# Zero products in TensorE's gaps, two product buffers in one tile, and one statistic for four heads, in cosine attention followed by a low-rank mixer

## The chip, the core and the metric

One core of one Trainium2 chip runs the kernel. The metric is the device time of one execution in microseconds, median of three runs: 604.58 us before (604.14 to 604.91). The core's engines work side by side, each through its own list of instructions in order: PE (TensorE: products and transposes), ACT (ScalarE), DVE (VectorE), POOL (GpSimd) and SP (SyncE); POOL and SP here issue most of the transfers. Semaphores order the engines among each other. PE writes its products to a memory of its own, PSUM, which has eight banks of 2 KB in each of 128 partitions.

## What is computed

Inputs q, k and v are (8, 12, 448, 64): batches, heads, tokens, width. The attention normalises q and k, and its output goes, heads side by side as 768 channels, through a low-rank mixing of tokens and a two-layer MLP on channels:

```python
q_n = q / (norm(q) + 1e-06);  k_n = k / (norm(k) + 1e-06)
scores = q_n @ k_n.T / tau
attn = softmax(scores)
x = (attn @ v) with the heads side by side        # (8, 448, 768)
u = x + (x.T @ U @ V).T                           # U: 448 x 32, V: 32 x 448
out = u + relu(u @ w_ch1) @ w_ch2                 # 768 -> 3072 -> 768
```

## The kernel before

Heads are taken in pairs, six pairs (0 to 5) in a batch, eight batches. In this text heads are also counted through all batches: head 12 is the first of batch 1. For each pair:

- Squares and sums (`squares`: ACT L455 or DVE L457, then DVE L461) give the squared norms of q and k. A logarithm and an exponential (ACT L474 and L477), an addition and a reciprocal (DVE L480 and L482) make the inverse norms. `stats` does this for a group of heads together; a group's small instructions wait for all of its sums.
- `norm` scales q and k (DVE L536, tile `xn`). In batches 0 and 1 PE transposes the result (L374, tile `tp`), twelve transposes a pair, eight of keys and four of queries, and ACT or DVE copies it to `qkT` (L826 or L828). From batch 2 on a transfer transposes.
- `attention` makes seven score products (PE L572) in three PSUM buffers `sc`, seven exponentials (ACT L577, tile `attn`), and for each head sixteen products with v (PE L594), four groups of four, which go to the PSUM buffer `av`. A column of ones in v makes the sums of the softmax. DVE takes their reciprocal (L601, tile `rd`) and multiplies (L603) into `X_sb`.

`av` is a ring of two buffers: a head takes the buffer of the head two back.

`stage0` mixes tokens (L625 to L700), and `mlp` does the two dense layers (L762 and L796, with relu at L785 and L787), whose products fill PE between those of the attention of the next batches.

The order of instructions is made by a planner in the kernel's own Python. Every operation is an `Op` with an engine, an expected duration, its dependencies, the ring slots that it takes and frees, and a priority. `Plan.run` walks through time, and gives a free engine the first operation that is ready: on PE and POOL from several streams, tried in the order in which they were made; on ACT, DVE and SP by priority. An `"ACT/DVE"` operation goes to whichever is free. The operations are then emitted in order of their planned starts, and waits between engines are put in by the framework below, from what each instruction reads and writes in each tile. The planner's durations are thus estimates that set an order; they do not appear in the program.

In the first pair the planner takes longer durations for PE: 0.31 for a score product (L572), 0.09 for a product with v (L594), 0.09 for a transpose (L557), where later ones have 0.19, 0.033 and 0.05. The start runs through `first`, `second`, `third` and `fourth`: loads of heads 0 to 2, 2 to 4, 4 to 8 and 8 to 12 of batch 0. The heads of `third` have two groups of statistics, 4 to 6 and 6 to 8 (L907 and L908).

Of the kernel before, what the change touches and what calls it, by code (L numbers as in the profile page):

```python
# [10 lines left out]
FP = mybir.dt.float32  # L11
BF = mybir.dt.bfloat16
# [192 lines left out]
def kernel(  # L205
# [12 lines left out]
    nc = tc.nc  # L218

    B, H, S, D = q.shape  # L220
# [11 lines left out]
    EPS = 1e-6  # L232
    PE_BATCHES = 2
    LATE, VLATE = 8.0, 3.2

    const = ctx.enter_context(tc.tile_pool(name="const", bufs=1))
    pool = ctx.enter_context(tc.tile_pool(name="pool", bufs=1))
    psum = ctx.enter_context(tc.tile_pool(name="psum", bufs=1, space=bass.MemoryType.PSUM))
# [8 lines left out]
    def ring(n, shape, dt, name, space=None):  # L247
        p = space or pool
        return Ring(n, lambda i: p.tile(shape, dt, name=name, tag=name, bufs=n))

    def fixed_ring(tiles):
        return Ring(len(tiles), lambda i: tiles[i % len(tiles)])
# [39 lines left out]
    r_rd = ring(2, [128, 4, 1], FP, "rd")  # L292
    r_mm = ring(3, [128, 512], FP, "mm", psum)
    r_sc = ring(3, [128, 512], FP, "sc", psum)
    r_av = ring(2, [128, 4, D + 8], FP, "av", psum)


    U_sb = const.tile([128, 2, 4, R], BF, name="U_sb")
    V_sb = const.tile([128, PAD + S + PAD], BF, name="V_sb")
    ident = const.tile([128, 128], BF, name="ident")  # L300
    w1_sb = const.tile([128, CC, F], BF, name="w1_sb")

    nc.scalar.preload_act_table_set("natural_log_exp_and_others")
# [13 lines left out]
    plan = Plan()  # L317
# [3 lines left out]
    pe_a = plan.stream("PE")  # L321
    pe_sc = plan.stream("PE")
    pe_mlp = plan.stream("PE")
    pool_q = plan.stream("POOL")

    def pe_t(n):
        return n / 2400.0 + 0.0025
# [14 lines left out]
    def fill(fn, n=256, prio=8, acq=(), deps=()):  # L342
        return plan.add(Op("DVE", 0.05 + n * 0.0005, fn, deps=deps, acq=acq, prio=prio))
# [46 lines left out]
    got, last_exp = {}, {}  # L390
# [95 lines left out]
    def stats(b, h0, h1, ld, ops, lo, hold=(), then=()):  # L486

        pr = 0.3 + 0.03 * h0 if b == 0 else 4
        inv = Slot(r_inv, h1 - h0)
        o, _ = scales(b, h0, h1, ld, ops, lo, (0, 1), inv, pr, "DVE" if b else "ACT/DVE", hold, then)  # L490
        for p in range(h0 // 2, h1 // 2):
            o_ = norm(b, p, ld, lo + 2 * p - h0, inv, 2 * p - h0, {0: o, 1: o}, pr)
        return o_
# [22 lines left out]
    def norm(b, p, ld, la, inv, a, deps, pr):  # L516


        by_pe = b < PE_BATCHES
        first = b == 0 and p == 0  # L520
        xn, qkT = Slot(r_xn, 3 if first else 2 if by_pe else 1), Slot(r_qkT, 7)
        need = [xn_set[count[0] % len(xn_t)]]
        count[0] += 1

        def part(i, h0=0, h1=2):
            def fn():
                n = h1 - h0
                src = ld.tile[:, i, la + h0:la + h1, :].rearrange("p h (c d) -> p h c d", d=D)
                sc = inv.tile[:, i, a + h0:a + h1, :].unsqueeze(3).to_broadcast([SCH, n, SC, D])
                if i == 0:  # L530
                    dst = xn.tile[:, 8:12, :].rearrange("p c (h d) -> p h c d", h=2)
                else:
                    dst = xn.tile.rearrange("p b e -> p (b e)")[:, 0:9 * 128].rearrange(
                        "p (h x) -> p h x", h=2)[:, h0:h1, 0:SC * 128].rearrange(
                        "p h (c e) -> p h c e", c=SC)[:, :, :, 0:D]
                nc.vector.tensor_mul(dst, src, sc)  # L536
            return plan.add(Op("DVE", dve_t(256 * (h1 - h0)), fn, deps=need + [deps[i]], acq=[xn],
                               rel=[getattr(ld, "slot", ld), inv], prio=pr))

        if first:  # L540
            ops = [part(0), part(1, 0, 1), part(1, 1, 2)]
            blocks = [(8, 12, ops[0]), (0, 4, ops[1]), (4, 8, ops[2])]
        else:
            ops = [part(1), part(0)]
            blocks = [(0, 8, ops[0]), (8, 12, ops[1])]
        if not by_pe:
            done = [plan.add(Op("SP", 0.1, lambda: nc.sync.dma_start_transpose(
                out=qkT.tile, in_=xn.tile.rearrange("p b e -> p (b e)")), deps=ops, acq=[qkT],
                rel=[xn], prio=0, lat=("x", 0.05 * 84, LATE)))]
        else:  # L550
            done = []
            for b0, b1, o in blocks:
                done.append(flip(
                    pe_tp, [(lambda z=z: xn.tile[:, z, :]) for z in range(b0, b1)], SCH,
                    lambda: qkT.tile, (lambda t_, x, b0=b0, b1=b1: key_tiles(t_, x, b0 // 4, b1 // 4)
                                   if b == 0 and b0 < 8 else [(t_[:, b0:b1, :], x)]),
                    [o], [qkT], [xn], 1, "ACT/DVE", 0.09 if first else 0.05, b == 0 and b0 < 8))  # L557
        got[b, p, "qkT"] = (qkT, lambda m: (done[:2] if m < 3 else done) if first else done, done)
        return ops


    def attention(b, p, X):
        off = PAD * (b % 2)
        qkT, qdeps, _ = got.pop((b, p, "qkT"))
        attn = Slot(r_attn, 2)
        exps = {}
        for m in (0, 1, 2, 6, 3, 4, 5) if b == 0 else range(7):
            sc = Slot(r_sc, 1)

            def score(sc=sc, m=m):  # L570
                kT = qkT.tile[:, 0:8, :].rearrange("p b s -> p (b s)")
                nc.tensor.matmul(out=sc.tile[:, 0:S], lhsT=kT[:, 128 * m:128 * (m + 1)],  # L572
                                 rhs=qkT.tile[:, 8:12, :].rearrange("p c s -> p (c s)"),
                                 start=True, stop=True)
            o = plan.add(Op("PE", 0.31 if b == 0 and p == 0 else pe_t(S), score, deps=qdeps(m), acq=[sc], rel=[qkT]),
                         pe_first if b == 0 else pe_sc)
            exps[m] = plan.add(Op("ACT", act_t(S), lambda sc=sc, m=m: nc.scalar.activation(  # L577
                out=attn.tile[:, m, off:off + S], in_=sc.tile[:, 0:S], func=AF.Exp,
                scale=inv_tau), deps=[o], acq=[attn], rel=[sc], prio=0.1 if b == 0 else 1))
        last_exp[b] = exps[5]  # L580
        if b == 0 and p == 0:
            last_exp["first"] = [exps[1]]
        muls = []
        for hh in range(2):
            h = 2 * p + hh
            av, rd = Slot(r_av, 1), Slot(r_rd, 1)
            mine = [3 * hh, 3 * hh + 1, 3 * hh + 2, 6] if b == 0 else [4 * hh, 4 * hh + 1, 4 * hh + 2, 3]
            need = [exps[m] for m in mine]
            for t in range(4):
                for j in range(4):  # L590
                    first, last = t == 0 and j == 0, t == 3 and j == 3
                    def fn(t=t, j=j, h=h, mine=mine, av=av):
                        m = mine[j]
                        nc.tensor.matmul(  # L594
                            out=av.tile[:, t, 0:D + 1],
                            lhsT=attn.tile[:, m, 128 * t:128 * (t + 1)],
                            rhs=v_t[b % 2][:, h, j, 0:D + 1], start=(j == 0), stop=(j == 3))
                    o = plan.add(Op("PE", 0.09 if b == 0 and p == 0 else 0.033, fn,
                        deps=need + got[b, h, "v"] + attn_set + [v_set[b % 2]] if first else (), acq=[av] if first else [],
                        rel=[attn] if last else []), pe_av)  # L600
            r = plan.add(Op("DVE", 0.20, lambda av=av, rd=rd: nc.vector.reciprocal(  # L601
                out=rd.tile, in_=av.tile[:, :, D:D + 1]), deps=[o], acq=[rd], prio=1))
            muls.append(plan.add(Op("DVE", dve_t(256), lambda av=av, rd=rd, h=h: nc.vector.tensor_mul(  # L603
                X.tile[:, :, h * D:(h + 1) * D], av.tile[:, :, 0:D],
                rd.tile.to_broadcast([128, 4, D])), deps=[r],
                acq=[X], rel=[av, rd], prio=1)))
        last_av[b, p] = o
        return muls
# [258 lines left out]
                       in_=V_f().rearrange("r (s c) -> r c s", c=SC))  # L867


    w2_ops = []  # L870
    NW = 4
    THIRDS = [(0, 4), (4, 8), (8, 12)]
# [6 lines left out]
    def att(b):  # L879
# [7 lines left out]
    first = lead, [plan.add(Op("SP", 0.45, lambda i=i, src=src: nc.sync.dma_start(  # L887
        out=lead.tile[:, i], in_=src[0, 0:2].rearrange("h (s c) d -> s h (c d)", c=SC)),
        acq=[uv], prio=-5, lat=2.5)) for i, src in enumerate((q, k))]
    second = load_qk(0, 2, 4, uses=2)  # L890
    third = load_qk(0, 4, 8)
# [7 lines left out]
    begun_2 = stats(0, 2, 4, *second, hold=begun[:2], then=begun)  # L899
# [4 lines left out]
    v0 = [plan.add(Op("SP", 0.45, lambda t=t: nc.sync.dma_start(out=V_f()[R * t:R * (t + 1)], in_=moe_V),  # L904
                      deps=[zf, *begun], prio=-2, lat=12.0)) for t in range(4)]
    u1 = load_u(1)
    stats(0, 4, 6, *third, hold=last_exp["first"], then=begun_2)  # L907
    stats(0, 6, 8, *third[:2], 2, hold=last_exp["first"], then=begun_2)  # L908
    late = stats(0, 8, 12, *fourth)
    load_w1(0, 6)  # L910
    load_w1(6, 12)
# [71 lines left out]
```

## Time and profile before

| what | us |
|---|---|
| median of three runs | 604.58 |
| the profiled execution, its own time | 604.58 |
| its span, first to last instruction | 602.7 |
| PE idle before its first instruction | 7.14 |
| first exponential of pair 0 (ACT L577) | 10.12 |
| first exponential of pair 2 | 20.47 |
| first product with v of head 4 | 29.84 |
| last exponential of batch 0 ends | 37.50 |
| dense products of line 762 start to run without a gap | 40.94 |
| last product with v (head 95) | 432 |

The rows of the groups by line for the two reads of `av`, and what ended the idle time before them:

```profile
L601 DVE RECIPROCAL rd<-av 128x4 f32<-128x4 f32 x96 | 17.0, 179 | 37.8 <-PE av L594 37.0
L603 DVE TENSOR_TENSOR X_sb<-av,rd 128x256 bf16<-128x256 f32 x96 | 40.1, 420 | 1.6
```

A row reads: line, engine, operation, what it writes and reads with shapes, how often; busy time in us and mean of one in ns; idle time of the engine just before, and what ended most of it. In a timeline a row is start, duration, engine, line, operation and how many are merged; in brackets the idle time before it and what ended it. In the chain of waits each row is start, duration and what the chain lay on. The page's clock row is the granted TensorE clock in tenths.

### The profile page before, as it was taken

The numbers are of one execution on the slowest core, as the hardware profiler recorded it, in microseconds if no ns is written. First come the engines' busy times: TensorE is split into PE (matmuls) and PEld (weight loads), VectorE is DVE, ScalarE is ACT, GpSimd is POOL, SyncE is SP. The second block draws the span as 40 slices with busy tenths as digits, with TensorE's granted clock in tenths as the row PEclk, the third lists the DMA queues.
The fourth block names the chain that finished last, engine by engine and source line by source line (L and its number), as shares of the span: only waits on it lengthen the run. The fifth ranks groups of instructions, "written<-read, shape, count | busy, mean of one in ns | idle before, by whom it ended". The sixth has DMA issues, their size and how long they took to land.

```text
span 602.7 us, 11511 instructions
## 1 busy us (share of the span) xinstructions
PE 584.3 (97%) x4702; PEld 346.8 (58%) x4725; DVE 300.8 (50%) x729; ACT 278.2 (46%) x601; POOL 114.9 (19%) x175
## 2 busy tenths in 40 slices
PE   4899999999999999999999999999999999999997
PEld 2566766555565665666445666566545666654465
DVE  8979849999988987654721244014300210110011
ACT  7867752477874377316741067505642025014300
POOL 8246334062703406000600000000000000000000
PEclk9999999999999999999999999999999999999999
DMA  9999999999998969715922142030002110310021
GB/s 134 201 181 118 202 202 121 166 132 144 148 173 114 180 105 147 111 53 94 121 27 66 53 73 47 1 93 27 15 1 53 52 40 1 89 43 1 0 53 54
DMA packets 150165, 54.81 MB, mean 91 GB/s; under 512 B 115040, under 2 KB 150112, under 8 KB 150112
## 3 DMA queue, kind: packets, MB, share of 16 engines
q0 software_dynamic: 72864, 25.73, 39.3%
q1 hardware_dynamic: 77184, 28.32, 25.8%
q8 instruction: 37, 0.61, 0.4%
q14 instruction: 16, 0.13, 0.1%
q10 hardware_dynamic: 64, 0.02, 0.0%
HBM read 52.25 MB, written 11.01 MB: 105 GB/s over the span
## 4 chain that ended last, share of the span: by engine, by line
PE 92%; DVE 4%; ACT 2%; issue 1%; DMA 0%; ACTq 0%
PE mm L796 36%; PE mm L762 34%; PE sc L572 10%; PE av L594 8%; PE mm L686 1%; DVE xn L536 1%; DVE ss L461 1%; ACT attn L577 1%; PE tp L374 1%; PE mm L651 1%; DVE qkT L828 1%; DMA raw_uv<-in_q_dram 0%; PE sc L762 0%; ACT relu L785 0%; PE sc L686 0%
## 5 line engine op out<-in xcount | busy, mean ns | idle before, releaser
L762 PE MATMUL mm<-uT,w_sb 128*128 128x384 bf16 (+1 forms) x1112 | 236.9, 353 | 1.2 <-ACT relu L785 0.2
L796 PE MATMUL mm<-w_sb,relu 128*128 128x384 bf16 (+1 forms) x1368 | 231.9, 324 | 0.3 <-DVE O_sb L805 0.3
L577 ACT ACTIVATE attn<-sc 128x448 bf16<-128x448 f32 x336 | 164.7, 547 | 108.9 <-PE av L594 55.5
L796 PEld LDWEIGHTS <-relu 128*128 128x128 bf16 x1368 | 132.6, 98 | 86.5 <-issue 0.2
L762 PEld LDWEIGHTS <-w_sb 128*128 128x128 bf16 x1152 | 112.1, 98 | 103.9 <-issue 1.4
L785 ACT ACTIVATE relu<-mm 128x512 bf16<-128x512 f32 (+1 forms) x158 | 86.6, 548 | 129.0 <-PE mm L762 128.3
L805 DVE TENSOR_TENSOR O_sb<-mm,u_nat 128x384 f32<-128x384 f32 (+1 forms) x57 | 31.1, 549 | 210.8 <-PE mm L796 207.5
L572 PE MATMUL sc<-qkT 128*128 128x448 bf16 x336 | 104.4, 361 | 3.9 <-ACT qkT L826 1.8
L594 PEld LDWEIGHTS <-attn 128*128 128x128 bf16 x1536 | 61.7, 98 | 16.9 <-issue 2.5
L418 POOL DMA_DIRECT2D v_nat<-in_v_dram x98 | 63.2, 656 | 32.6 <-DMA w_sb<-in_moe_w_ch_dram 15.6
L594 PE MATMUL av<-v_nat,attn 128*128 128x65 bf16 x1536 | 65.3, 194 | 0.5 <-DVE X_sb L603 0.5
L461 DVE TENSOR_REDUCE ss<-sq 112x8 f32<-112x512 bf16 x96 | 63.2, 673 | 0.4 <-ACT sq L455 0.3
L536 DVE TENSOR_TENSOR xn<-qk_nat,inv 112x512 bf16<-112x512 bf16 x94 | 61.0, 681 | 1.3 <-DMA qkT<-xn 1.1
L396 POOL DMA_DIRECT2D qk_nat<-in_q_dram x24 | 17.2, 716 | 134.6 <-DVE xn L536 73.0
L603 DVE TENSOR_TENSOR X_sb<-av,rd 128x256 bf16<-128x256 f32 x96 | 40.1, 420 | 1.6
L572 PEld LDWEIGHTS <-qkT 128*128 128x128 bf16 x336 | 28.3, 98 | 21.8 <-issue 5.6
L601 DVE RECIPROCAL rd<-av 128x4 f32<-128x4 f32 x96 | 17.0, 179 | 37.8 <-PE av L594 37.0
L457 DVE TENSOR_TENSOR sq<-qk_nat 112x512 bf16<-112x512 bf16 x87 | 33.6, 413 | 0.0
L700 DVE TENSOR_TENSOR u_nat<-mm,X_sb 128x384 bf16<-128x384 f32 x36 | 19.1, 552 | 14.4 <-PE mm L686 14.2
L787 DVE TENSOR_SCALAR relu<-mm 128x384 bf16<-128x384 f32 (+1 forms) x31 | 18.7, 604 | 12.7 <-PE mm L762 12.2
L474 ACT ACTIVATE ln<-ss 112x32 f32<-112x32 f32 (+2 forms) x27 | 6.4, 235 | 30.2 <-DVE ss L461 30.1
L374 PE MATMUL tp<-ident,xn 112*128 112x112 bf16 x144 | 11.6, 227 | 7.9 <-DVE xn L536 7.5
(61 smaller groups left out, 169.8 us busy)
## 6 DMA issues: line engine op xcount, KB each, us to landing
qk_nat<-in_q_dram POOLq DMA_DIRECT2D x23, 224.0 KB, 5.6
qk_nat<-in_k_dram POOLq DMA_DIRECT2D x23, 224.0 KB, 6.9
w_sb<-in_moe_w_ch_dram POOLq DMA_DIRECT2D x4, 1152.0 KB, 14.2
w_sb<-in_moe_w_ch_dram POOLq DMA_DIRECT2D x8, 576.0 KB, 16.6
out_dram<-O_sb SPq DMA_DIRECT2D x15, 168.0 KB, 2.3
out_dram<-O_sb SPq DMA_DIRECT2D x16, 144.0 KB, 2.1
out_dram<-O_sb SPq DMA_DIRECT2D x16, 120.0 KB, 2.0
out_dram<-O_sb SPq DMA_DIRECT2D x16, 96.0 KB, 2.2
```

What stands on the lines that cost most here:

```text
L418: nc.gpsimd.dma_start(out=vb[p0:p0 + s1 - s0, hs, j, 0:D], in_=v[b, hs].rearrange("h (s c) d -> c s h d", c=SC)[c, s0:s1]),
L457: nc.vector.tensor_mul(y, x, x)
L461: lambda i=i, a0=a0, a1=a1, sq=sq: nc.vector.reduce_sum(ss.tile[:, i, a0:a1, :].rearrange("p h c -> p (h c)"), sq.tile[:, 0:a1 - a0, :].re ...
L536: nc.vector.tensor_mul(dst, src, sc)
L572: nc.tensor.matmul(out=sc.tile[:, 0:S], lhsT=kT[:, 128 * m:128 * (m + 1)], rhs=qkT.tile[:, 8:12, :].rearrange("p c s -> p (c s)"), start=T ...
L577: exps[m] = plan.add(Op("ACT", act_t(S), lambda sc=sc, m=m: nc.scalar.activation(out=attn.tile[:, m, off:off + S], in_=sc.tile[:, 0:S], fu ...
L594: nc.tensor.matmul(out=av.tile[:, t, 0:D + 1], lhsT=attn.tile[:, m, 128 * t:128 * (t + 1)], rhs=v_t[b % 2][:, h, j, 0:D + 1], start=(j == ...
L603: muls.append(plan.add(Op("DVE", dve_t(256), lambda av=av, rd=rd, h=h: nc.vector.tensor_mul(X.tile[:, :, h * D:(h + 1) * D], av.tile[:, :, ...
L762: o = plan.add(Op("PE", pe_t(n), lambda cc=cc: nc.tensor.matmul(out=mm.tile[:, 0:n], lhsT=w1_sb[:, cc, f * 128:(f + 1) * 128], rhs=uT.tile ...
L785: nc.scalar.activation(out=relu.tile[:, f, 0:n], in_=mm.tile[:, 0:n], func=AF.Relu)
L796: nc.tensor.matmul(out=mm.tile[:, 0:c1 - c0], lhsT=relu.tile[:, f, i * 128:(i + 1) * 128], rhs=w2_t[:, f, c0:c1], start=(f == 0), stop=(f ...
L805: nc.vector.tensor_add(out=O.tile[:, 0:w], in0=mm.tile[:, 0:w], in1=us[i].tile[:, c0:c1]),
```

## The change

Three things are changed.

1. The two `av` buffers, so far two tiles of a ring, become the two halves of one tile of two banks. A head still takes the half of the head two back.
2. A tile `warm` of zeros is set by DVE, and 75 products of it with itself, 208 columns wide, are given to PE in a stream of their own, tried last: they are planned wherever no other stream is ready. They write the unused tail of the second bank. At the same time the longer durations of the first pair leave the plan.
3. Heads 4 to 8 of batch 0 have one group of statistics in place of two.

```diff
     LATE, VLATE = 8.0, 3.2
+    WARM = 75
...
-    r_av = ring(2, [128, 4, D + 8], FP, "av", psum)
+    av_t = psum.tile([128, 2, 512], FP, name="av", tag="av", bufs=1)
+    r_av = fixed_ring([av_t[:, i, 0:4 * (D + 8)].rearrange("p (t d) -> p t d", t=4) for i in range(2)])
...
+    warm = const.tile([128, 208], BF, name="warm")
...
+    pe_warm = plan.stream("PE")
...
-                    [o], [qkT], [xn], 1, "ACT/DVE", 0.09 if first else 0.05, b == 0 and b0 < 8))
+                    [o], [qkT], [xn], 1, "ACT/DVE", 0.05, b == 0 and b0 < 8))
...
-            o = plan.add(Op("PE", 0.31 if b == 0 and p == 0 else pe_t(S), score, deps=qdeps(m), acq=[sc], rel=[qkT]),
+            o = plan.add(Op("PE", pe_t(S), score, deps=qdeps(m), acq=[sc], rel=[qkT]),
...
-                    o = plan.add(Op("PE", 0.09 if b == 0 and p == 0 else 0.033, fn,
+                    o = plan.add(Op("PE", 0.033, fn,
...
+    warm_set = fill(lambda: nc.vector.memset(warm, 0.0), 100, prio=-9)
+    for i in range(WARM):
+        plan.add(Op("PE", 0.18, lambda i=i: nc.tensor.matmul(
+            out=av_t[:, 1, 304:512], lhsT=warm[:, 0:128], rhs=warm, start=(i == 0), stop=True,
+            skip_group_check=True), deps=[warm_set]), pe_warm)
...
-    stats(0, 4, 6, *third, hold=last_exp["first"], then=begun_2)
-    stats(0, 6, 8, *third[:2], 2, hold=last_exp["first"], then=begun_2)
+    stats(0, 4, 8, *third, hold=last_exp["first"], then=begun_2)
```

In the order that this gives, 36 of the 75 zero products stand ahead of the first transpose, and the last one just before the transposes of pair 2. The order of instructions on each engine is another one up to the end of batch 0's attention, and again the same as before from the dense products on, but for a few swaps in batch 1. POOL and SP keep their order throughout. The lines of the changed kernel that are named in this text are four further down up to the new products: L594 is L598 there, L601 and L603 are L605 and L607.

## The prediction

> **What bounds the kernel now.** I read the busy shares first, then the groups by line, the chain of waits, the timeline of the first 45 us, and last the timeline around each place where a head's product is read. TensorE is the bound as a whole.
>
> ```profile
> PE 584.3 (97%) x4702; PEld 346.8 (58%) x4725; DVE 300.8 (50%) x729; ACT 278.2 (46%) x601; POOL 114.9 (19%) x175
> PEclk9999999999999999999999999999999999999999
> ```
>
> PE is idle for 602.7 − 584.3 = 18.4 us, 7.14 of them before its first instruction. So later on whatever holds PE is paid in full. The clock row claims full speed throughout, but the durations do not:
>
> ```profile
> 8.90 1.30 PE L572 MATMUL sc<-qkT 128*128 128x448 bf16 x3 [0.26 <-ACT qkT L826]
> 12.43 1.32 PE L374 MATMUL tp<-ident,xn 112*128 112x112 bf16 x12
> 18.41 0.56 PE L374 MATMUL tp<-ident,xn 112*128 112x112 bf16 x8
> 20.08 0.73 PE L572 MATMUL sc<-qkT 128*128 128x448 bf16 x3 [0.59 <-ACT qkT L826]
> ```
>
> Up to 18 us PE is slow: a score product takes 0.37 us on the chain of waits up to 17.5 us and 0.19 from 31.92 on; transposes go from 0.10 each, (1.32 − 0.23) / 11, to 0.05, (0.56 − 0.19) / 7. Only a part of this slow stretch lies on the chain:
>
> ```profile
> 14.67 1.30 PE sc L572 x3
> 16.47 0.37 PE sc L572
> 19.00 0.76 DVE qkT L828 x3
> ```
>
> From 14.67 to 18.98 the chain lies on PE (4.3 us); before and after it lies on ACT and DVE. That bounds what a faster PE can give. Three marks of this stage are used below:
>
> ```profile
> 16.73 1.29 DVE L536 TENSOR_TENSOR xn<-qk_nat,inv 112x512 bf16<-112x512 bf16 x2
> 20.47 1.42 ACT L577 ACTIVATE attn<-sc 128x448 bf16<-128x448 f32 x3
> 29.84 1.18 PE L594 MATMUL av<-v_nat,attn 128*128 128x65 bf16 x32 [0.19 <-DVE X_sb L603]
> ```
>
> They are pair 2's normalised operands, pair 2's first exponentials, and head 4's product with v. Then the place that decides, here at the start of batch 5 (heads are counted through, 12 a batch; this is head 60 on):
>
> ```profile
> 266.98 1.18 PE L594 MATMUL av<-v_nat,attn 128*128 128x65 bf16 x32
> 267.70 0.18 DVE L601 RECIPROCAL rd<-av 128x4 f32<-128x4 f32 x1
> 267.91 0.42 DVE L603 TENSOR_TENSOR X_sb<-av,rd 128x256 bf16<-128x256 f32 x1
> 268.25 0.17 DVE L601 RECIPROCAL rd<-av 128x4 f32<-128x4 f32 x1
> 268.36 0.56 DVE L700 TENSOR_TENSOR u_nat<-mm,X_sb 128x384 bf16<-128x384 f32 x1
> 268.84 0.41 DVE L603 TENSOR_TENSOR X_sb<-av,rd 128x256 bf16<-128x256 f32 x1
> 269.46 0.67 PE L594 MATMUL av<-v_nat,attn 128*128 128x65 bf16 x16
> 270.17 0.18 DVE L601 RECIPROCAL rd<-av 128x4 f32<-128x4 f32 x1 [0.92 <-PE av L594]
> 270.39 0.42 DVE L603 TENSOR_TENSOR X_sb<-av,rd 128x256 bf16<-128x256 f32 x1
> ```
>
> Heads 60 and 61 run on PE without a gap (32 products), and DVE reads head 60 while PE writes head 61: two buffers at work.
>
> **The change, part by part.** *One tile for the two av buffers.* The two buffers become halves of one tile. In the built programs the waits differ: before, 54 instructions of L594 wait for a read (L601 or L603), each for the head two back, whose buffer they take. After, 87 wait for a read of the head just before, which lies in the other half; and reads wait for products of the next head that stand ahead of them. So a product that stands behind a read in the program's order now waits for it. By the times of this trace, in 60 of the 87 the read is done when PE arrives; in 27 it is not.
>
> Prices, from these rows: a product's start to the read's start is 0.23 (head 12: last product 63.02, read 63.25); the reciprocal takes 0.18, the multiplication 0.42, 0.03 between them, and 0.055 from DVE's end to PE (31.31 to 31.37). A wait for a reciprocal behind one's own product: 0.23 + 0.18 + 0.055 = 0.465. For a multiplication: 0.705. For both: 0.915. Off each go 0.034, the step between products, and 0.19 for every score product between.
>
> Batch 5: the reciprocal of head 60 now stands between products 7 and 8 of head 61, so 0.465 − 0.034 = 0.43. Its multiplication waits for product 15 of head 61, then come reciprocal 61, L700 and multiplication 61, which head 62 waits for: end 270.10 against PE's 269.89, 0.25. Head 63 waits for reciprocal 62, 0.04, and between its products 4 and 5 for multiplication 62, 0.67. Sum 1.4, and batches 6 and 7 repeat this timeline (rows at 346 and 409 us): 4.2. Batch 4: 0.90 (DVE is late itself, reciprocal 48 ends at 206.02), then 0.22, 0.04, 0.12, 0.67: 1.9. Batch 3: 0.43 in head 39, 0.2 to 0.4 at head 45: 0.7. Batch 2: nothing, all reads are done 0.7 us or more ahead. Batch 1: 0.41 (head 15), 0.06, 0.43 (head 17), 0.68 (head 19): 1.6. Together **8.4 us**, paid in full because PE is busy 15.71 of 16 us (62 to 78) and 15.00 of 15 (200 to 215, 260 to 275). If DVE's lateness of batch 1 and 4 shrinks while PE stands still, 6; if held reads hold DVE's other work, 10.
>
> Batch 0, heads 4 to 11, in the order of the built program: mid-head multiplications of heads 3, 4, 5, 7 and 9 at 0.48, 0.67, 0.67, 0.67, 0.67; reciprocals of heads 4, 5, 7 at 0.24, 0.43, 0.24; both reads of heads 6, 8, 10 less what PE does between, 0.69, 0.18, 0.34. Sum **5.3 us**. PE is full here from 32 to 40 us. The other end is half of it, 2.6, if PE would have waited for exponentials anyway (ACT is 2.00 of 2.00 busy at 34 to 36); I take 5.3, since the held products stand ahead of the scores that ACT needs.
>
> *Zeros, cold costs taken out of the plan, and four heads' statistics at once (L907/908).* These only reorder the first 50 us; POOL's and SP's queues hold the same order, so no DMA is moved past another. The warm tile's memset (about 0.12, as the 0.09 to 0.27 of its neighbours) fits into the 0.29 that DVE idles before 4.40; uncovered it costs itself. 36 zero products of 208 columns stand ahead of the first transpose: 208/448 of 0.37 = 0.17 each, 6.2 us from about 1.05 on, so 7.3 at worst against 7.14; the 39 others at 0.08 to 0.17 lie in PE's gaps. The four small instructions that merging saves (0.3 and 0.2 on ACT, 0.17 and 0.24 on DVE) are gain that the walk contains.
>
> The walk, with rows of this trace in the new order: ACT copies the first query (0.53) and half keys (0.61) from 7.51 to 8.65; first exponential at 9.1 instead of 10.12. Then ACT meets the second pair's logarithm, whose second sum DVE now does behind a memset, a sum and three key copies (0.48 + 0.64 + 0.5 + 0.64 from 7.99): 10.25 against 9.97. Pair 0's exponentials end at 13.55 instead of 13.87 (one square went behind them). Pair 1's operands come at 12.05 to 13.35 instead of 11.44 to 12.72, its query copy behind two sums at 15.0, its exponentials at 15.45 instead of 15.34. The gain is spent, though PE is fast. Heads 4 to 8 need all four sums (16.66), a logarithm behind exponentials, and DVE's squares and sums of heads 8 to 12 in between: operands of pair 2 at 19.9 instead of 16.73, of pair 3 done at 22.4; pair 2's query is copied behind these, so its exponentials start at 23.45 instead of 20.47, 3.0 later. Pair 3 is then ready, and ACT no longer idles as it did at 24.5, 26.4 and 29.2: head 4's product starts behind reciprocal 3 at 30.7 instead of 29.84, **0.9 later**. Bounds: −2.1 (half of the 4.3 us that the chain lies on a slow PE) to +3.0 (nothing made up); I take the walk, which contains every instruction.
>
> Two pages bear on this. The Trainium skill, "PSUM — Partial Sum Buffer", section "Summary: rules for kernel authors", wants a read during matmuls in another bank, guarded by bank; the halves are two banks, so by it no wait was needed and the sum would be the 0.9 alone, but the built program's waits decide. "TensorE: Matmul & The Clock Gate", section "Part 4: PE-mode transpose", says that transposes do not get the full clock; the rows above (0.10 to 0.05) contradict it, and by it the first transposes would stay about 0.5 us slower.
>
> **Sum.** 602.7 (span) + 0.9 + 5.3 + 8.4 = 617.3; the execution's own time, 604.58, is also the median and 1.9 above its span: **619.2 us**.
>
> **Rivals.** *A: half of it is absorbed.* PE would have waited for exponentials in batch 0, and DVE catches up while PE is held: 604.6 + 0.5 + 2.6 + 6 = 613.7, down to 611.1 when the start gains the 2.1 instead. For: ACT and DVE are both near 2.00 of 2.00 until 36 us. Against: PE is full from 32 us. *B: the held reads hold DVE.* Sums, relus and u additions queue behind a reciprocal that waits for PE, and DVE is 14.07 of 16 us busy at 62 to 78, 13.96 of 15 at 200 to 215: 10 instead of 8.4, and 3.0 at the start: 604.6 + 3.0 + 5.3 + 10 = 622.9, some 625 if heads 20 to 47 lose their slack of 0.7. Against: batches 5 to 7, DVE under half busy. *C: faster.* PE starts fast, the chain's 4.3 us on PE halve, and the waits prove void because reads run ahead of PE: 604.6 − 2.1 = 602.5. It decides only if the products show no idle time ended by a read. Against: 27 reads end too late by this trace. *D: the zeros do not warm PE.* 7.3 instead of 7.14, and transposes and scores as slow as now, which lie under ACT: 619 to 620, inside the forecast.
>
> **How the numbers follow.** The forecast with D 0.60 (own range 615.5 to 622), A 0.21, B 0.12, C 0.04, and 0.03 that gain and loss cancel. The range 611 to 623.5 takes in A and the nearer part of B. About 0.2% (1.2 us) is what a measurement here can tell from no change: faster 0.04, same 0.02, slower 0.94.
>
> **What would show it.** Right: idle time of PE ahead of L598 released by L605 and L607, some 13 us in all against 1.0 now; two consecutive heads never 32 products without a gap; PE at the dense product of line 762 (now 40.94) near 47; a score product of 0.19 us from the first on. Wrong: no such idle time, or pair 2's first exponential before 21 us; then the walk or the waits are at fault, and the time lies under 612.

## The result, and the profile after

The changed kernel takes 618.36 us (617.14 to 619.47), the kernel before beside it 604.51 (604.14 to 604.91): ratio 1.0229, 95% interval 1.0207 to 1.025. The profiled execution took 619.47 us, 1.8 of it outside its span of 617.7.

The busy shares and the clock row of the changed kernel's page:

```profile
PE 595.9 (96%) x4777; PEld 355.6 (58%) x4800; DVE 302.1 (49%) x727; ACT 279.1 (45%) x600; POOL 114.0 (18%) x175
PEclk9879999999999999999999999999999999999999
```

PE is busy 11.6 us longer than before (595.9 − 584.3), of which the 75 zero products are 10.9, and yet the span grew by 15.0, although zeros now fill most of the 7.14 us that PE idled at the start (its first instruction comes at 1.03). So PE also stands idle more, later on. Where, the groups by line tell (busy and mean, then idle time ahead and what ended it), the products with v of the kernel before first:

```profile
L594 PE MATMUL av<-v_nat,attn 128*128 128x65 bf16 x1536 | 65.3, 194 | 0.5 <-DVE X_sb L603 0.5
L598 PE MATMUL av<-v_nat,attn 128*128 128x65 bf16 x1536 | 68.9, 195 | 9.4 <-DVE X_sb L607 6.3
L607 DVE TENSOR_TENSOR X_sb<-av,rd 128x256 bf16<-128x256 f32 x96 | 40.3, 421 | 7.5 <-PE av L598 6.1
L605 DVE RECIPROCAL rd<-av 128x4 f32<-128x4 f32 x96 | 17.0, 179 | 47.3 <-PE av L598 46.6
```

The products with v have the same duration as before, but 9.4 us of idle time ahead of them in place of 0.5, of which 6.3 (14 times) ended with a multiplication and, in the query by line, 2.4 (7 times) with a reciprocal. The multiplications in turn now wait 6.1 us for products; before they waited 1.6 in all. PE and DVE wait for each other, in turn. The timeline at the start of batch 5, where the prediction showed 32 products without a gap (rows left out):

```profile
278.29 0.93 PE L598 MATMUL av<-v_nat,attn 128*128 128x65 bf16 x24
...
279.26 0.18 DVE L605 RECIPROCAL rd<-av 128x4 f32<-128x4 f32 x1 [0.21 <-PE av L598]
279.49 0.41 PE L598 MATMUL av<-v_nat,attn 128*128 128x65 bf16 x8 [0.27 <-DVE rd L605]
...
282.23 0.32 PE L598 MATMUL av<-v_nat,attn 128*128 128x65 bf16 x5
...
282.58 0.42 DVE L607 TENSOR_TENSOR X_sb<-av,rd 128x256 bf16<-128x256 f32 x1 [0.41 <-PE av L598]
283.06 0.51 PE L598 MATMUL av<-v_nat,attn 128*128 128x65 bf16 x11 [0.52 <-DVE X_sb L607]
```

Head 60 and eight products of head 61 run, and then PE stops for the reciprocal of head 60, which reads the other half of the tile. The 24th product starts at 278.29 + 0.93 − 0.19 = 279.03, the next at 279.49: 0.46, less the step of 0.034 is 0.43. The stop inside head 63 is 283.06 − 282.36 − 0.034 = 0.67. Both are the prediction's prices to the hundredth. The bracket shows only 0.27 and 0.52 because it counts from the modelled end of a product, 0.16 later than the next one could have started. So the 8.7 us in 21 waits (6.3 and 2.4) are 8.7 + 21 × 0.16 = 12.1 us of standing still.

In batch 0 something else joins in. Stretches of 2 us: PE, PEld, DVE, ACT, POOL busy (with the number of instructions), then the granted clock, DMA share and GB/s:

```profile
34.00:36.00 2.00, 1.12 (x12) 0.70 (x12) 0.90 (x3) 0.54 (x1) 1.65 (x3) 0.77 1.06 157
36.00:38.00 2.00, 1.74 (x15) 1.01 (x14) 0.41 (x2) 1.48 (x3) 0.00 (x0) 0.50 1.11 190
38.00:40.00 2.00, 1.75 (x15) 0.96 (x14) 0.68 (x3) 0.74 (x3) 0.00 (x0) 0.50 1.17 205
40.00:42.00 2.00, 2.00 (x17) 1.08 (x17) 0.12 (x1) 1.48 (x3) 0.35 (x1) 0.52 1.42 198
```

After some microseconds of stops the clock falls to half for 35 to 42 us; before, the row read 1.00 there. The four timed runs differ with it: spans of 615.4, 616.1, 617.1 and 617.7 at mean clocks of 1.000, 0.997, 0.994 and 0.992.

The start itself lost nothing: head 4's first product comes at 29.54, before at 29.84. The last product of head 11 comes at 45.65 against 38.04.

### The profile page after: what moved, and what is told of

It reads as the page before. It is cut to its first block, busy times and chain, and to the rows that moved or that the text cites. A ratio compares the mean times of both kernels' runs of the same rounds, so it can differ in the third digit from the quotient of the medians.

```text
span 617.7 us, 11681 instructions
## 1 busy us (share of the span) xinstructions
PE 595.9 (96%) x4777; PEld 355.6 (58%) x4800; DVE 302.1 (49%) x727; ACT 279.1 (45%) x600; POOL 114.0 (18%) x175
## 4 chain that ended last, share of the span: by engine, by line
PE 88%; DVE 6%; ACT 2%; DMA 2%; issue 1%; POOL 1%; ACTq 0%; DVEq 0%; POOLq 0%
PE mm L800 33%; PE mm L766 33%; PE sc L576 10%; PE av L598 8%; DVE xn L540 1%; PE mm L690 1%; DMA v_nat<-in_v_dram 1%; DVE X_sb L607 1%; DVE ss L465 1%; ACT attn L581 1%; DMA qk_nat<-in_q_dram 1%; DVE sq L461 1%; PE mm L655 1%; PE tp L378 1%; PE sc L766 0%
## 5 line engine op out<-in xcount | busy, mean ns | idle before, releaser
L598 PEld LDWEIGHTS <-attn 128*128 128x128 bf16 x1536 | 63.5, 99 | 28.7 <-issue 12.9
L598 PE MATMUL av<-v_nat,attn 128*128 128x65 bf16 x1536 | 68.9, 195 | 9.4 <-DVE X_sb L607 6.3
L607 DVE TENSOR_TENSOR X_sb<-av,rd 128x256 bf16<-128x256 f32 x96 | 40.3, 421 | 7.5 <-PE av L598 6.1
L605 DVE RECIPROCAL rd<-av 128x4 f32<-128x4 f32 x96 | 17.0, 179 | 47.3 <-PE av L598 46.6
L400 POOL DMA_DIRECT2D qk_nat<-in_k_dram x24 | 16.9, 702 | 3.8 <-DMA w_sb<-in_moe_w_ch_dram 3.6
## 6 DMA issues: line engine op xcount, KB each, us to landing
w_sb<-in_moe_w_ch_dram POOLq DMA_DIRECT2D x4, 1152.0 KB, 14.6
```

The source lines that it names most:

```text
L400: ops = [load(lambda i=i, src=src: nc.gpsimd.dma_start(out=ld.tile[:, i, lo:lo + h1 - h0, :], in_=src[b, h0:h1].rearrange("h (s c) d -> s ...
L598: nc.tensor.matmul(out=av.tile[:, t, 0:D + 1], lhsT=attn.tile[:, m, 128 * t:128 * (t + 1)], rhs=v_t[b % 2][:, h, j, 0:D + 1], start=(j == ...
```

## The experiments

Theory: the framework orders reads and products by tile, so with both halves in one tile a product waits for a read of the other half, and that is all that costs. Rival: the start costs (zeros, the planner's new order, one group of statistics). All times below stand beside the kernel before on the same chip, 604.6 to 604.8.

### Taking the merge back, and making it alone

Two tiles in the changed kernel; every engine keeps its order:

```diff
-    av_t = psum.tile([128, 2, 512], FP, name="av", tag="av", bufs=1)
+    av_t = [psum.tile([128, 512], FP, name=f"av{i}", tag=f"av{i}", bufs=1) for i in range(2)]
...
-            out=av_t[:, 1, 304:512], lhsT=warm[:, 0:128], rhs=warm, start=(i == 0), stop=True,
+            out=av_t[1][:, 304:512], lhsT=warm[:, 0:128], rhs=warm, start=(i == 0), stop=True,
```

> The changed kernel with two tiles for the two product buffers in place of one; zeros, costs in the plan and the single statistic stay, and every engine keeps the order of the changed kernel. Theory (waits for a read that lies in the other half): idle time of PE ahead of the products with v that a read ended falls from 8.7 us to under 1.5, the stretch of half clock at 35 to 42 us goes, head 4 still starts near 29.5, and the time is 602.5 to 605.5. Rival (the reordered start, or the zeros, cost): the time stays above 611, or between 606 and 611 if they share the cost.

Measured: 603.78 us (603.37 to 604.95), ratio 0.9987, interval 0.9978 to 0.9996. Head 4 starts at 29.68, and the granted clock reads 1.00 from 29 to 47 us: without the stops there is no half clock there. Its row in the groups by line, and its timeline at batch 5:

```profile
L598 PE MATMUL av<-v_nat,attn 128*128 128x65 bf16 x1536 | 65.7, 194 | 1.2 <-DMA v_nat<-in_v_dram 1.0
```

```profile
267.49 1.18 PE L598 MATMUL av<-v_nat,attn 128*128 128x65 bf16 x32
```

No read ends an idle time of PE any more, and the 32 products run on. The whole loss is the merge, 618.4 − 603.8 = 14.6.

The merge alone, in the kernel before:

```diff
-    r_av = ring(2, [128, 4, D + 8], FP, "av", psum)
+    av_t = psum.tile([128, 2, 512], FP, name="av", tag="av", bufs=1)
+    r_av = fixed_ring([av_t[:, i, 0:4 * (D + 8)].rearrange("p (t d) -> p t d", t=4) for i in range(2)])
```

> The kernel before with nothing but its two product buffers merged into one tile; every engine keeps the order of the kernel before. Theory: batches 1 to 7 lose 7.6 us as in the changed kernel, batch 0 loses 3 to 8, time 614 to 620. Rival (the start costs): no more than 607.

Measured: 616.33 us (615.69 to 616.92), ratio 1.019, interval 1.0175 to 1.0205. Groups by line (products with v are one line further down here):

```profile
L595 PE MATMUL av<-v_nat,attn 128*128 128x65 bf16 x1536 | 68.3, 195 | 7.8 <-DVE X_sb L604 5.0 <-DVE rd L602 2.6
```

Same waits, without zeros or anything else of the change. The rival falls.

### The zeros left out

`WARM = 0` in the changed kernel, with one tile, and then with two:

> The changed kernel without its zero products. Theory: the waits stay, so 617 to 621; PE is slow up to about 18 us again, which costs at most 2. Rival (zeros in PE's list are what costs, by the work itself or by the clock that falls after them): 614 or less.

Measured: 621.83 us (620.27 to 622.21), ratio 1.0283, interval 1.0266 to 1.03. The waits stay, as the theory wants, but the kernel lost 3.5 us more, where I had put at most 2 on a slow PE.

> Two tiles, one group of statistics, the shorter costs in the plan, but no zero products: the kernel that lost 17 us with one tile (621.8), with two. Theory: all of that was waits for reads in the other half, so 603 to 605.5 (head 12 within 1 us of 62.5), and a slow PE before 18 us costs at most 1.5 against the same with zeros (603.8). Rival (this order is bad in itself, by its batch 1): above 608.

Measured: 604.81 us (603.4 to 605.68), ratio 0.9999, interval 0.999 to 1.0009. With two tiles the same order is as good as before, so the additional loss is the merge as well: 17.0 us in this order. Its planner has laid the heads of batch 1 differently against the reads: by the starts of the products, six heads in a row (13 to 18) are stopped in their middle, once by 0.43 us and five times by 0.67 or 0.68. In the changed kernel two of that batch were, by 0.43 and 0.68.

### The zeros alone, and the planned zeros without the zeros

The kernel before with the 75 zero products as its only change (two tiles, two groups, the longer costs kept):

> The kernel before with the 75 zero products in planned gaps as its only change (two tiles, two groups of statistics, the longer costs of the first pair kept). Theory (ACT and DVE set the start, a fast PE is hidden there): 604 to 605.5, first score products at 0.19 us. Rival (the 4.3 us of the chain on a slow PE are worth something): 602 to 603.5.

Measured: 603.20 us (602.95 to 603.82), ratio 0.9975, interval 0.9965 to 0.9985. The rival's range; a fast PE seemed to be worth 1.5 us. So the same program, with the zeros counted by the planner and not issued:

```diff
-        plan.add(Op("PE", 0.18, lambda i=i: nc.tensor.matmul(
-            out=av_t[1][:, 304:512], lhsT=warm[:, 0:128], rhs=warm, start=(i == 0), stop=True,
-            skip_group_check=True), deps=[warm_set]), pe_warm)
+        plan.add(Op("PE", 0.18, lambda: None, deps=[warm_set]), pe_warm)
```

> The run with zeros only, in which the planner still counts 75 zero products but none is issued: every engine keeps the order of that run, and PE has no zeros. If the fast PE is the gain (603.2 against 604.7), it is gone: 604.2 to 605.5, first score products at 0.35 us again. If the order that the planned zeros bring is the gain, it stays: 602.8 to 603.7.

Measured: 603.21 us (602.8 to 604.99), ratio 0.9979, interval 0.9969 to 0.9988. The gain stays without a single zero: it is the order. The first score products and pair 1's first exponentials, with zeros issued and then without, from the two timelines:

```profile
8.91 0.74 PE L576 MATMUL sc<-qkT 128*128 128x448 bf16 x3
...
15.10 1.39 ACT L581 ACTIVATE attn<-sc 128x448 bf16<-128x448 f32 x3
```

```profile
9.08 1.30 PE L576 MATMUL sc<-qkT 128*128 128x448 bf16 x3 [0.26 <-ACT qkT L830]
...
15.08 1.40 ACT L581 ACTIVATE attn<-sc 128x448 bf16<-128x448 f32 x3
```

Three score products take 0.74 us with a fast PE and 1.30 with a slow one, and ACT's exponentials of the next pair stand at the same time. The two tiles of a full bank and the setting of `warm`, which this run also has, are in the kernel of 604.81 us above too, and gain nothing there. A part of what the order gains is seen on ACT later. The kernel before, pairs 3 and 4, and then the run with the zeros planned and not issued:

```profile
25.01 1.42 ACT L577 ACTIVATE attn<-sc 128x448 bf16<-128x448 f32 x3 [0.51 <-PE av L594]
26.95 0.53 ACT L826 COPY qkT<-tp 128x448 bf16<-128x448 bf16 x1 [0.53 <-PE tp L374]
...
30.45 1.42 ACT L577 ACTIVATE attn<-sc 128x448 bf16<-128x448 f32 x3 [1.21 <-PE av L594]
```

```profile
27.11 1.03 ACT L830 COPY qkT<-tp 128x672 bf16<-128x672 bf16 x3
28.00 2.76 ACT L581 ACTIVATE attn<-sc 128x448 bf16<-128x448 f32 x6
31.52 0.54 ACT L581 ACTIVATE attn<-sc 128x448 bf16<-128x448 f32 x1 [0.76 <-PE sc L576]
```

Three waits of ACT for PE, 2.25 us together, are gone: transposes and scores stand elsewhere among the products with v. Two new ones, 0.76 and 0.21 us, stand in their place, and batch 0's exponentials end 0.42 us earlier, at 37.07. The two profiled spans differ by 0.9 us, so this is not all of the gain; where the rest lies was not followed.

### The other parts of the start

The changed kernel with two tiles and two groups of statistics:

> Two tiles, zeros and shorter costs as in the changed kernel, but two groups of statistics for heads 4 to 6 and 6 to 8 as before. Theory: no waits for reads; pair 2's operands come earlier than 19.4 us and its first exponential near 21; with a PE at full speed from the start head 4 begins up to 2 us earlier: 602.5 to 604.5. Rival (ACT and DVE set the start whatever PE does): 604 to 606, no faster than with one group.

Measured: 605.23 us (604.41 to 605.96), ratio 1.0006, interval 0.9997 to 1.0016. That is the rival's range. Pair 2's first exponential came at 19.86, sooner than expected, and bought nothing; ACT's three waits of the kernel before are there again (0.68, 0.52 and 1.20 us).

Zeros alone, and one group of statistics:

> The run with zeros only, and one group of statistics for heads 4 to 8 in place of two. By the prediction's walk (pair 2's operands come 3 us later and are made up by head 4): 603.2 to 604.5, pair 2's first exponential at 22.5 or later. If one group saves time for itself, as it does by 1.4 us with the shorter costs (603.8 against 605.2): 601.5 to 602.7.

Measured: 603.98 us (603.71 to 606.09), ratio 0.9996, interval 0.9986 to 1.0005; pair 2's first exponential at 22.81, both as in the first of the two expectations. So one group costs 0.8 in the one order and saves 1.4 in the other (605.2 to 603.8), and the shorter costs lose 2.0 (603.2 to 605.2). These parts act through the order alone, and their effects do not add up.

Two tiles, and zeros enough to fill PE's gap at 18.5 to 20.3 us (`WARM = 110`):

> Two tiles with 110 zero products in place of 75, so that PE's gap ahead of pair 2's transposes at 18.5 to 20.3 us is filled. If that gap is what lets the granted clock fall to half (0.56 and 0.59 at 22 to 26 us with 75 zeros), the clock stays at 1.00 there, and heads 2 to 4 come up to 1 us earlier: 602.5 to 603.8. If it does not depend on the gap, the half clock stays and the time is 603.5 to 605; zeros that hold up later products would give 604.5 or more.

Measured: 605.29 us (604.33 to 605.76), ratio 1.0008, interval 0.9998 to 1.0017. The same stretch with two tiles and 75 zeros, and with 110:

```profile
22.00:24.00 2.00, 1.97 (x10) 0.83 (x9) 2.00 (x6) 1.88 (x6) 0.00 (x0) 0.56 1.27 217
```

```profile
22.00:24.00 2.00, 1.30 (x12) 0.78 (x11) 1.77 (x5) 2.00 (x7) 0.33 (x1) 1.00 1.27 220
```

PE's other products have the same order in both up to 23 us. With 75 zeros PE idles for 1.82 us and the clock falls (0.56); with the gap filled up to 0.83 us it stays (1.00). So here the gap let it fall. Yet nothing is gained: PE only idles more, 0.70 of 2 us, since ACT is full there. The time is higher by 1.5; part of it may be zeros and reads that wait for each other, for the zeros write the second tile (they waited 1.5 us for reads, reads 1.3 for them). The profiled spans differ by only 0.2, so this is not settled.

### The merge in a third order

Zeros alone with the merge:

> The run with zeros only, and its two product buffers merged into one tile; same order. The merge cost 11.6 us in the order of before, 14.6 in that of the changed kernel, 17.0 in that without zeros. Theory (price set by how the order lays products against reads, 7 us or so of it in batches 1 to 7): 613 to 618. Rival (the merge is dear only beside a disturbed start): under 610.

Measured: 615.38 us (615.30 to 615.45), ratio 1.0177, interval 1.0162 to 1.0192. With this there are four pairs of profiles that differ in the merge alone. What it adds, in us, from the starts of products with v in each batch (each column from the last product of the batch before to the last of its own; heads up to 11: last product of head 11; clock: granted mean at 29 to 47 us with one tile):

| order of | heads to 11 | batch 1 | 2 | 3 | 4 | 5, 6, 7 each | sum | clock |
|---|---|---|---|---|---|---|---|---|
| prediction | 5.3 | 1.6 | 0 | 0.7 | 1.9 | 1.4 | 13.7 | |
| changed kernel | 6.95 | 1.25 | 0 | 0.86 | 1.74 | 1.25 | 14.55 | 0.81 |
| kernel before | 4.98 | 0.85 | 0 | 0.85 | 1.73 | 1.25 | 12.15 | 0.91 |
| changed, no zeros | 4.95 | 3.63 | 0.66 | 0.70 | 1.70 | 1.24 | 15.35 | 1.00 |
| zeros alone | 5.34 | 0.52 | 0 | 0.86 | 1.75 | 1.25 | 12.22 | 1.00 |

Three of the four keep one order from head 20 on, the one without zeros comes to it at head 60: where the order is the same, so is the price, within 0.02 us. The profiled run without zeros was the shortest of its four (span 618.5 at a mean clock of 0.997, the others 620.0 to 620.4 at 0.993 or 0.994), which is why its row adds up to 15.35 and not to the 17.0 of the medians. In batch 0 it is 5.0 to 5.3 in the two with a full clock, also 5.0 in the kernel before, whose clock was at half for 3.4 us (0.91), and 6.95 in the one whose clock was at half longest, 6.8 us.

### One buffer that the planner knows of

The kernel before with a ring of one buffer (`ring(1, ...)` in place of `ring(2, ...)`), and the changed kernel with only the first half handed out (`range(1)`):

> The kernel before with one product buffer in place of two, so that the planner itself knows that a head's products must wait for the reads of the head before, and plans dense products between two heads. Theory (the merged tile is dear because the waits stand in places that the planner left unfilled, not because one buffer is too few): batches 1 to 7 lose less than 1.5 us in all, batch 0, which has no dense products to fill with, 2 to 5: 606 to 611. Rival (the wait itself costs, wherever it stands): 614 or more, as with the merge alone (616.3).

Measured: 611.80 us (611.15 to 613.82), ratio 1.0129, interval 1.0108 to 1.0151.

> The changed kernel, in which only the first half of the merged tile is handed out, so that the planner knows of the wait. Same theories: 605 to 611 against the changed kernel's 618.4, or 614 and more.

Measured: 613.17 us (612.35 to 614.07), ratio 1.0143, interval 1.0127 to 1.0159. Both fall between the two expectations. Waits of PE's products with v for a read between 50 and 450 us (us in total, times, longest), first the merge alone, then one buffer:

```profile
PE av L595 <- DVE rd L602: 2.4, 7, 0.7
PE av L595 <- DVE X_sb L604: 2.3, 5, 0.5
```

```profile
PE av L594 <- DVE X_sb L603: 0.2, 1, 0.2
```

From batch 1 on the theory holds for these waits: with dense products planned between two heads, twelve become one. It was a little too hopeful for the sum. PE's idle time from 48 to 595 us is 4.95, against 3.10 before: 1.85 more, where less than 1.5 was expected, and three waits for DVE's tile `O_sb` make up 2.4 of the 4.95. (With the merge it is 6.49, which counts each wait 0.16 too short.)

The larger part of the loss lies in the start, which has little to plan in between: some 5 us, the 7.0 by which the profiled spans differ less 1.85. Head 11's last product comes at 44.44, against 38.04 with two buffers and 43.01 with the merge, but the order is another one. That is the upper end of what I had allowed (2 to 5), or above it. A part may be a slow PE: three score products at 19.79 still took 1.28 us, and the first record of a full clock stands at 27.23 us, before at 18.32. In the changed kernel with one half it stands at 6.74, and head 11's last product is hardly earlier, at 44.25; how much is the clock's was not separated.

## Why the prediction was right

The forecast of 619.2 us stood 0.8 above the median, by the cause that it named. That it came so near is in part luck: its terms were off in both directions, two too high and one too low by up to 1.7 us, and cancelled.

*False waits in batches 1 to 7, 8.4 us.* Right; 7.6 measured. The places are those predicted, and the prices too: 0.43 and 0.67 to the hundredth. So is the 0.90 in batch 4. The rest are small waits, and most came out shorter: head 62 waited 0.08 in place of 0.25, so that each of the last three batches lost 1.25 in place of 1.4, and head 15 waited 0.14 in place of 0.41, so that batch 1 lost 1.25 in place of 1.6.

*False waits of heads 4 to 11, 5.3 us.* The term fits the waits themselves, 4.95 and 5.34 where the clock was full. It was too small for the changed kernel, 6.95, most likely since the prediction had no term for a clock that falls when PE keeps stopping. The difference, 1.6 to 2.0, is of the size that the timed runs vary with their clock (2.3: the run at 1.000 was the shortest). No run held the clock up in the changed kernel's order, so this is argued and not shown. The low end, that ACT would absorb half, was wrong, and rival A with it: the held products stood ahead of the scores, and ACT waited too, 3.3 us in three waits for PE's scores between 31.9 and 36.3 us.

*The start up to head 4, +0.9.* Wrong in sign: head 4 came 0.3 earlier, and with two tiles the whole rest of the change gains 0.8 us by the ratio (0.9978 to 0.9996, so 0.2 to 1.3). The walk had the parts right within about half a microsecond up to pair 2, operands at 19.9 against 19.38 and first exponential at 23.45 against 23.09 measured. Its failing step is the next one, that only 2.1 of the 3.0 us would be made up. Pair 3 came 1.9 late (26.90 against 25.01), pair 4 0.3 (30.76 against 30.45), because ACT idled only 0.24 us there, where it had idled 2.25.

*The fast PE.* The prediction bounded it by 2.1 us and took the walk, in which it was hidden. That was right, more sharply than I knew: with the same order, zeros issued or not, 603.20 and 603.21. This was tested in the order of the run with zeros alone; in the changed kernel's own order it was not. Rival C's ground (the chain's 4.3 us on a slow PE) was empty in that order: the chain of waits names what came last, not what would come earlier.

*Signs.* PE idle ahead of L598 by reads showed 8.7, not 13, since the row counts from modelled ends; corrected by 0.16 for each of 21 waits it is 12.1. The dense products of line 762 start to run without a gap at 48.55, not near 47, by the low term of heads 4 to 11. "Never 32 products without a gap" was too strong: heads 12 and 13 run through at 69.99, heads 36 and 37 at 165.16, since both of a pair are read behind the last of their products. Rival B did not show: batch 2 lost nothing. Rival D falls by the first score products, 0.19 us each (three in 0.73 us at 8.79).

The Trainium skill's "PSUM — Partial Sum Buffer", section "Summary: rules for kernel authors", would have it that reads in another bank, guarded by bank, go on beside products. Here the halves were two banks and the guard was by tile, and that cost 11.6 to 17.0 us; with a guard of its own for each bank (two tiles) the cost was gone.

The fastest version is the kernel before with the zeros in its plan, issued or not: 603.2 us, 1.5 less than before and 15.2 less than the changed kernel.

## What to carry to other kernels

Buffers that two engines use in turn have to be separate tiles for whatever puts in the waits: two banks in one tile turned double buffering into hand-over, and the program stayed correct and in the same order, so only the waits show it. If buffers must share a tile, tell the planner: one buffer that it knew of (611.8) was better than two halves that it took for independent (616.3). Before an engine is made faster, take its speed away and keep the order; here that showed that a gain of 1.5 us came with the order and not with the speed.

## What the runs showed of the hardware

The clock row of the kernel before shows nines where three score products took 1.30 us. Its trace has no clock record ahead of 18.32 us, the time up to which PE was slow, and the row stands at full speed until the first record. So at the start durations are to be read, not the row.

PE got its full clock 3.3 us after its first zero product in the changed kernel (at 1.03 us, full from 4.36 in the trace's clock records). Over the eight traces with zeros issued, all from 1.03 us on, it took 3.0 to 5.9 us; in the six without, where PE starts near 7 us and has gaps, the record comes at 15.7 to 27.2 us.

The clock fell to half at 21.43 us in the changed kernel, after a gap of 1.97 us (18.1 to 20.1), and again at 35.08, when PE had no gap over 0.6 us but was busy 1.39 of 2 us and less. In all five traces in which PE idled 1.3 to 2.4 us in one piece near 18 to 20 us, the clock fell 0.3 to 1.9 us later; where none there was longer than 1.0 us, it stayed. But two gaps of 1.46 and 1.49 us at 5.8 to 7.3 us (two tiles with 110 zeros, and the zeros alone) left it at full, so the length of a gap alone does not decide.

The Trainium skill, "TensorE: Matmul & The Clock Gate", section "Part 1: The HAM clock gate", has full speed follow a busy window of about 3.4 us, and half speed an idle one. The full clock after 3.3 us is near that, the spread up to 5.9 less so; the fall after a gap of 1.97 us does not fit. What decides is open: the zeros alone with the merge had much the same stops (PE busy 1.41 and 1.36 of 2 us at 32 to 36, where the changed kernel had 1.39 and 1.12) and kept 1.00 in all its runs, which then lay within 0.15 us of each other.
